# Second FFN stage in two passes of 26 products of three row groups, with its weights streamed

## The chip, the core and the metric

The kernel runs on one core of one Trainium2 chip. The metric is device microseconds from start to end of one execution. The kernel before takes 1042.76 us (median of 3 runs, 1042.61 to 1042.82). The engines named here are PE (TensorE matmul), DVE (VectorE), ACT (ScalarE) and SP (SyncE, which issues nearly all DMAs). Each takes its own instructions strictly in the order in which the program wrote them; they are tied together by semaphores.

## The reference

```python
scores = scale * np.matmul(q, k.transpose(0, 1, 3, 2)) - np.log(S)     # 8 batches, 12 heads, S = 448, D = 64
attn = 1.0 / (1.0 + np.exp(-scores))
x = np.matmul(attn, v)               # then (8 * 448, 768)
h = x @ w_in                         # 768 -> 2048
g = np.maximum(0.01 * h, h)
return g @ w_out                     # 2048 -> 768
```

All inputs are float32. The second FFN stage is the last product, `g @ w_out`.

## The kernel before

Three stages follow each other on PE: sigmoid attention over 48 pairs of heads, the first FFN stage (`h`, four passes of two batches each) and the second FFN stage (four passes of two batches each). A float32 product is made from three fp32r products: each operand is split into a high part (a cast, on ACT) and a low part (the value less its high part, on DVE), and high by high, high by low and low by high are summed in PSUM. So each operand that PE reads costs one ACT and one DVE instruction first.

Both FFN stages use fewer block products than the plain scheme, at the price of sums of blocks. The first one has 7 products for 8. The second one (`PRODUCTS`, L48) cuts `g` of two batches in 8 blocks, and `w_out` in blocks and sums of blocks, and has 20 products for the plain 24. A row of `PRODUCTS` names a stored form of `w_out`, a PSUM accumulator ("chain" A to E), the operand made of `g` (a block, or a sum or difference of two), and the results that read the chain's partial sum once the product is done. One product is 2 halves of 12 matmuls of 128 by 448 columns.

**Preparation of the weights** (`prep`, L367). Both weight matrices come as float64 bits. DVE turns them into float32 (five instructions on each of four pieces of a unit) and forms sums of blocks: `firsts` (L316) for `w_in`, `second` (L327) for `w_out`. Raw blocks and sums are stored to DRAM (`t0`, `t1`) and read back by the stages. There are 8 units of `w_in`, then 8 of `w_out`. A unit's converted blocks (`wd`) and its sums (`ws`) each take one of the two buffers of tag "w", so the next unit's `wd` takes the buffer of this unit's `wd`. `prep` is a generator: each `yield` ends one DVE instruction or is an empty step; `WAIT` = 9 empty steps follow each unit. In the attention stage `prepare` (L424) takes steps at the rate of `PACES` for the five slots of a round (one round is two pairs of heads), as long as an estimate of DVE's queue leaves room; in the first FFN stage `fill` (L432) takes up to four steps per half product. It thereby settles at which place of DVE's order each preparation instruction stands, between those of attention (`qks`, the low part of q and k of a later pair, and `x`, one of the two copies of the result out of PSUM).

**The sums of `g`**. The first FFN stage stores `g` to DRAM (`gd`), with six sums or differences of blocks (`MADE`) so that the second stage need not make these.

**The second stage's order**. `use` lists 7 triples of forms of `w_out` for 4 row units; each is loaded and split once, and stays in SBUF for all four passes. Nine of these 28 tiles (`AHEAD`) are loaded and split while PE still works in the first FFN stage, with four operands (`READY`). Then for each half product `work` (L1011) records in order: sums, low and high parts of the operands two or three ahead, weights not yet loaded, the reads of the product just ended (`read`, L983), and the 12 matmuls. `g_load` (L920) issues the loads of `g` on SP, up to eight half products ahead. Results are stored by SP one slot after the last read of them.

PSUM has three double banks for chains A to C and two single ones; a chain takes the one that was given back first. The first product takes the double bank 0.

## Time and profile before

| | |
|---|---|
| median of the runs | 1042.76 us |
| the profiled execution | 1043.02 us, its span (first to last instruction) 1041.2 us |
| granted PE clock | 1.000 |
| PE busy | 1036.3 us (100%) |
| DVE busy | 817.6 us (79%) |
| ACT busy | 592.9 us (57%) |
| DMA | 294.92 MB, mean 283 GB/s |
| attention | 0 to 250.0 us |
| first FFN stage | 250.0 to 653.3 us |
| second FFN stage | 653.3 to 1037.4 us, then the last reads and stores |

Views of the profile that are quoted later: "groups" has a row for all instructions of one kind with their count, then busy us and mean ns of one, then the idle time before them; "timeline" has a start, a duration, the instruction and, in brackets, the idle time before it with what ended it; "stages" has for each stretch the busy us of PE, PE's weight loads, DVE, ACT and POOL with the number of instructions, then clock, DMA share and GB/s; "DMA issues" has count, KB of each and the median us from issue to landing.

### The profile page before, as it was taken

How to read it: one execution, taken by the hardware profiler on the slowest of the kernel's cores; microseconds unless marked ns; L12 is line 12 of the kernel's file. 1: busy time of each engine (PE TensorE's matmuls, PEld its weight loads, DVE VectorE, ACT ScalarE, POOL GpSimd, SP SyncE). 2: the span in 40 equal slices, each digit the busy share in tenths (PEclk: the TensorE clock that was granted, in tenths of full speed). 3: DMA queues.
4: the chain of work that ended last, by engine and by line, in shares of the span. 5: the costliest groups of instructions: out<-in, count | busy, mean ns of one | idle time of the engine just before them, and what ended most of it. 6: DMA issues, size and time to landing. Idle time of an engine off the chain costs nothing.

```text
span 1041.2 us, 15783 instructions
## 1 busy us (share of the span) xinstructions
PE 1036.3 (100%) x5786; PEld 872.3 (84%) x5786; DVE 817.6 (79%) x1081; ACT 592.9 (57%) x706; POOL 0.3 (0%) x5
## 2 busy tenths in 40 slices
PE   9999999999999999999999999999999999999998
PEld 5545555556999999999999999999999999999997
DVE  4778888678988898889666558899876797678675
ACT  6778787777545555555555555566354345434442
POOL 0000000000000000000000000000000000000000
PEclk9999999999999999999999999999999999999999
DMA  8888787878789798889767898999976796688674
GB/s 301 285 280 288 256 282 260 295 251 293 259 299 314 267 326 295 305 306 346 247 228 251 285 352 286 368 352 333 335 252 223 274 340 223 233 292 286 219 268 173
DMA packets 115837, 294.92 MB, mean 283 GB/s; under 512 B 11568, under 2 KB 41264, under 8 KB 115760
## 3 DMA queue, kind: packets, MB, share of 16 engines
q1 hardware_dynamic: 114032, 290.01, 79.7%
q10 hardware_dynamic: 1728, 3.90, 1.0%
q8 instruction: 46, 0.75, 0.3%
q14 instruction: 31, 0.25, 0.1%
HBM read 207.22 MB, written 86.64 MB: 282 GB/s over the span
## 4 chain that ended last, share of the span: by engine, by line
PE 99%; ACT 0%; ACTq 0%; DVE 0%; DVEq 0%; issue 0%
PE px_h L110 22%; PE pv L110 13%; PE sc L110 11%; PE acc_B L110 11%; PE acc_A L110 11%; PE pz_h L110 11%; PE acc_D L110 6%; PE acc_C L110 6%; PE py_h L110 6%; PE acc_E L110 4%; ACTq L110 0%; ACT L110 0%; DVE o L110 0%; ACT qks L110 0%; DVEq L1086 0%
## 5 line engine op out<-in xcount | busy, mean ns | idle before, releaser
L110 PE MATMUL px_h<-hi,w 128*128 128x448 f32 x768 | 223.2, 361 | 0.0
L110 PEld LDWEIGHTS px_h<-hi,w 128*128 128x128 f32 x768 | 143.9, 187 | 11.3 <-issue 0.7
L110 DVE TENSOR_TENSOR w<-wx,w 128x768 fp32r<-128x768 f32 x112 | 106.9, 954 | 45.0 <-ACT w L110 45.0
L110 PE MATMUL px_h<-lo,w 128*128 128x448 f32 x384 | 139.4, 363 | 0.0
L110 ACT ACTIVATE s<-sc 128x896 f32<-128x896 f32 x144 | 119.5, 934 | 9.7 <-PE sc L110 9.7
L110 ACT CAST gh<-gf 128x896 fp32r<-128x896 f32 x72 | 67.7, 945 | 86.5 <-DVE gf L110 43.1
L110 ACT CAST gh<-g 128x896 fp32r<-128x896 f32 x80 | 74.1, 942 | 74.3 <-PE acc_A L110 21.8
L110 PE MATMUL pv<-s,v 128*64 128x448 f32 x576 | 113.8, 543 | 0.0
L110 PE MATMUL pz_h<-hi,w 128*128 128x448 f32 x384 | 112.7, 361 | 0.0
L110 PE MATMUL acc_A<-gh,w 128*128 128x448 f32 x384 | 111.4, 361 | 0.0
L110 PE MATMUL acc_B<-gh,w 128*128 128x448 f32 x384 | 110.8, 361 | 0.0
L110 PEld LDWEIGHTS sc<-qks 64*128 64x128 f32 x876 | 80.7, 189 | 23.1 <-issue 16.9
L110 DVE TENSOR_TENSOR g<-g,gh 128x896 fp32r<-128x896 f32 x80 | 85.6, 1087 | 18.3 <-ACT gh L110 17.0
L110 PE MATMUL sc<-qks 64*128 64x448 f32 (+1 forms) x876 | 95.6, 369 | 0.1
L110 DVE TENSOR_TENSOR gf<-g,g 128x896 f32<-128x896 f32 x80 | 86.9, 1087 | 9.3 <-DMA g<-g 2.7
L110 ACT ACTIVATE c_h<-c_h 128x896 f32<-128x896 f32 x48 | 45.8, 954 | 81.4 <-DVE c_h L110 81.4
L110 PEld LDWEIGHTS pv<-s,v 128*64 128x64 f32 x576 | 39.1, 137 | 63.3 <-issue 53.9
L110 ACT CAST w<-wx 128x768 fp32r<-128x768 f32 x112 | 91.4, 833 | 0.0
L110 DVE TENSOR_TENSOR g<-gf,gh 128x896 fp32r<-128x896 f32 x72 | 78.2, 1086 | 2.3 <-ACT gh L110 2.0
L110 PEld LDWEIGHTS acc_A<-gh,w 128*128 128x128 f32 x384 | 72.0, 188 | 5.4
L110 PEld LDWEIGHTS acc_B<-gh,w 128*128 128x128 f32 x384 | 71.9, 187 | 5.4
L110 PEld LDWEIGHTS pz_h<-hi,w 128*128 128x128 f32 x384 | 71.9, 187 | 5.3
(79 smaller groups left out, 1701.3 us busy)
## 6 DMA issues: line engine op xcount, KB each, us to landing
g<-g SPq DMA_DIRECT2D x200, 448.0 KB, 5.2
wx<-t SPq DMA_DIRECT2D x112, 384.0 KB, 4.9
g<-c_h SPq DMA_DIRECT2D x60, 448.0 KB, 4.3
qk<-in_qk SPq DMA_DIRECT2D x46, 448.0 KB, 5.1
g<-s SPq DMA_DIRECT2D x45, 448.0 KB, 5.2
wr<-in_w_in SPq DMA_DIRECT2D x32, 384.0 KB, 4.6
wr<-in_w_out SPq DMA_DIRECT2D x32, 384.0 KB, 4.3
out<-o SPq DMA_DIRECT2D x23, 448.0 KB, 3.3
```

Source lines behind the costliest of these rows:

```text
L110: return lambda *args, **kw: tc.keep_in_program_order(issue(*args, **kw))
```

## The change

The second stage now takes four batches in a pass and has two passes. A pass has 26 products of 24 forms of `w_out`. One product covers three row groups of 128 at once (`m` in 0 to 2) and all four units `e` of the contraction, so it has 3 x 4 x 3 = 36 matmuls of 128 by 448. The two chains A and B ("lanes") alternate, each with one PSUM tile of three banks; most products add to what the lane holds (third field False), and a result reads a lane between two products. An operand is a sum of up to three stored blocks or sums, or of the operand of one or two products before (`<1`, `<2`).

The weights of a product are one tile of 128 x 1536. It is loaded for each of the 52 products anew, five products ahead, and split into high (ACT) and low (DVE) each time. Six tiles are in turn: three (`t2a`) stand free in the first FFN stage and are filled and split there, three (`t2b`) lie in memory that the first FFN stage gives back. Two operands (`READY`) are made beforehand.

`second` forms eight sums into `ws`, changes two blocks of `wd`, stores both, takes nine empty steps, changes all eight blocks of `wd` in place, and stores `wd` again: 18 DVE instructions of 192 elements for nine of 128 to 256. `PACES` are about 1.35 times as large. The first FFN stage makes 5 sums of `g` for an even and 8 for an odd pass, where it made 6.

```diff
-AHEAD = 9
-GG, OO, FAR, SPARE = 10, 8, 8, 3
-READY, LEAD = 4, 2
-
-PACES = 4, 5, 4.2, 2.8, 2
+AHEAD, FAR, SPARE = 5, 6, 1
+GG, OO, WW = 7, 8, (3, 3)
+READY, LEAD = 2, 2
+
+PACES = 5.5, 6.5, 5.5, 3.7, 2.7
 TIMES = 1.92, 1.92, 2.33, 2.33, 1.66
...
+STEPS = (
+    ("sum", "s0", 1, "d1", -1, "d7"), ("sum", "s1", -1, "d2", 1, "d4"), ("sum", "s2", -1, "d2", -1, "d3"),
...
+    ("sum", "s6", -1, "d5", 1, "s3"), ("sum", "s7", -1, "s1", 1, "s0"), ("sum", "d2", 1, "d2", -1, "d0"),
+    ("sum", "d7", -1, "d6", -1, "d7"), ("store", "s", 0, 8, 0), ("store", "d", 0, 8, 8), ("wait",),
+    ("sum", "d5", 1, "d7", 1, "d5"), ("sum", "d6", -1, "d2", -1, "d6"), ("sum", "d4", -1, "d4", -1, "d5"),
...
+    ("sum", "d3", 1, "d5", -1, "d6"), ("sum", "d1", -1, "d2", 1, "d1"), ("store", "d", 0, 8, 16))
...
+        for what, *x in STEPS:
+            if what == "wait":
+                yield from (None for _ in range(WAIT))
+            elif what == "store":
+                side, i, n, form = x
+                dma(out=t2d[:, form:form + n, e, at:at + size], in_=both[side][:, i:i + n])
...
+    psum = banks("ps_o", dict(A=(1, 3), B=(1, 3), one=(2, 1)))
...
+    for k in range(total):
+        p, i = divmod(k, NF)
+        _, lane, begins, _, reads = PRODUCTS[i]
+        ending = k == total - 1
         def work():
...
+            for x in operands[k:k + 3]:
+                if x.hi and not x.has_low:
+                    x.low()
+            if k:
+                read(k - 1)
+            for x in operands[k:k + 4]:
+                if x.x is None:
+                    x.whole()
+                    x.high()
+            for x in weights[WW[0]:k + 4]:
+                if k and not x.has_high:
+                    x.high()
+                elif x.has_high and not x.has_low and x.k < k + 3:
+                    x.low()
...
+            for m in range(NM):
+                todo = [(e, part, n) for e in range(KQ) for part, n in ((0, 0), (0, 1), (1, 0))]
+                acc = accs[lane][0][m]
                 for at, (e, part, n) in enumerate(todo):
-                    mm(banks_of[m], lhsT=w2[g, h * KS + e].of(form, part, m), rhs=(me.hi, me.lo)[n][:, e],
-                       start=begins and at == 0, stop=h == 1 and at == len(todo) - 1, skip_group_check=True)
+                    mm(acc, lhsT=w.of(part, e, m), rhs=(me.hi, me.lo)[n].t[:, e],
+                       start=begins and at == 0, stop=at == len(todo) - 1, skip_group_check=True)
...
+            if WW[0] <= k + AHEAD < total:
+                weights[k + AHEAD].load()
+            g_load(k)
```

How this moves instructions is shown at three places. In these rows the name left of the arrow is written and the one right of it read; DVE_49, PE_49, Activation_49 and DMAHW0_49 to DMAHW7_49 are the semaphores that the instruction waits for, the last eight those of DMAs.

The first place is DVE in the attention stage, in the middle of the preparation of the first unit of `w_out`. Before, from the last sums of the unit to the next unit:

```order
L110 TENSOR_TENSOR ws1_0_2333<-wd1_0_2190 128x2x128
L110 TENSOR_TENSOR ws1_0_2333<-ws1_0_2333 128x2x128 [waits DVE_49]
L110 TENSOR_TENSOR ws1_0_2333<-wd1_0_2190,ws1_0_2333 128x2x128
L110 TENSOR_TENSOR ws1_0_2333<-ws1_0_2333,wd1_0_2190 128x128 [waits DVE_49]
L110 TENSOR_TENSOR ws1_0_2333<-ws1_0_2333 128x128
L110 TENSOR_TENSOR qks_40_2423<-qk_40_2271,qks_40_2423 128x832 [waits DMAHW3_49,PE_49,Activation_49]
```

Now, from the last sum into `ws` over the two changed blocks of `wd`, the nine empty steps and the changes in place:

```order
L127 TENSOR_TENSOR ws1_0_2091<-ws1_0_2091 128x192
L127 TENSOR_TENSOR wd1_0_1922<-wd1_0_1922 128x192
L127 SCALAR_TENSOR_TENSOR wd1_0_1922<-wd1_0_1922 128x192 [waits DVE_49]
L127 TENSOR_TENSOR wd1_0_1922<-wd1_0_1922 128x192 [waits DMAHW7_49,DVE_49]
L127 TENSOR_TENSOR qks_34_2129<-qk_34_1979,qks_34_2129 128x832 [waits DMAHW6_49,PE_49,Activation_49]
L127 SCALAR_TENSOR_TENSOR wd1_0_1922<-wd1_0_1922 128x192
L127 SCALAR_TENSOR_TENSOR wd1_0_1922<-wd1_0_1922 128x192 [waits DVE_49]
L127 TENSOR_TENSOR wd1_0_1922<-wd1_0_1922 128x192
L127 SCALAR_TENSOR_TENSOR wd1_0_1922<-wd1_0_1922 128x192 [waits DVE_49]
L127 TENSOR_TENSOR qks_35_2148<-qk_35_2044,qks_35_2148 128x832 [waits DMAHW1_49,PE_49,Activation_49]
```

The fourth of these rows is the first one after the empty steps. It waits for a DMA semaphore, that of the second store; no other DVE instruction stands between it and the row before it, and the low parts of two pairs of heads stand behind it.

The second place is SP where the first FFN stage ends. It now reads, from the last store of this stage on SP to the loads of the second stage's weights (`g` are loads of operands, `t1` the stored forms of `w_out`):

```order
L127 DMA g_3_15_123<-s7_3_2_6269 128x896 [waits DMAHW4_49,DVE_49]
L127 DMA g1s0_2_6350<-g_1_8_87 128x1792 [waits DMAHW6_49,PE_49]
L127 DMA g111_3_6421<-g_1_5_84 128x1792 [waits DMAHW2_49]
L127 DMA g001_4_6423<-g_0_1_67 128x1792 [waits DMAHW3_49]
L127 DMA g011_4_6425<-g_0_5_71 128x1792 [waits DMAHW1_49,DMAHW5_49,DMAHW0_49,DMAHW7_49,DVE_49,Activation_49]
L127 DMA g1s4_4_6427<-g_1_12_91 128x1792 [waits DMAHW4_49]
L127 DMA g1s7_5_6429<-g_1_15_94 128x1792 [waits DMAHW5_49,DMAHW2_49]
L127 DMA w1_3_6431<-t1_61 128x1536 [waits DMAHW3_49,PE_49]
L127 DMA w1_4_6433<-t1_61 128x1536
L127 DMA w1_5_6476<-t1_61 128x1536
```

The weights of the fourth product, `w1_3`, stand behind three loads of operands, the first of which (`g011_4`, into memory that the first FFN stage gives back) waits for four DMA semaphores. These are of the last stores of the first FFN stage, which are on ACT's queue (`ends` in `after`).

The third place is SP at the very end, where the last results are stored:

```order
L127 DMA out_0<-o1_010_7747 128x224 [waits DMAHW0_49,DVE_49]
L127 DMA out_0<-o1_010_7747 128x224 [waits DMAHW2_49,DVE_49]
L127 DMA out_0<-o1_010_7747 128x224 [waits DMAHW4_49,DVE_49]
L127 DMA out_0<-o1_000_8383 128x3x448 [waits DMAHW6_49]
L1125 UNCONDITIONAL_BRANCH
```

Before, the last row ahead of the branch was a piece of 128 x 224; now a whole result, `o1_000`, follows the three pieces of the last product.

More of the change, by code (lines that the diff above doesn't have):

```diff
@@ L652, in advance, with __init__ @@
             at_load += 1
+    class Results(dict):
+        def __init__(self):
+            self.planned = set()
     class First:
@@ L709, in after @@
             z = LATER if u == NU // 2 - 1 else 0
-            for i, x in enumerate(x for x in MADE if name(row, col) in x and set(x.replace("-", "+").split("+")) <= set(c)):
-                later(2 + i + z, lambda x=x: made(x))
+            have = set(c)
+            i = 0
+            for x in MADE[p % 2]:
+                if x[0] not in c.planned and {x[2], x[3]} <= have | c.planned:
+                    c.planned.add(x[0])
+                    later(2 + i + z, lambda x=x: made(*x))
+                    i += 1
     last = B * NP - 1
@@ new lines, in whole, with free, release @@
+            for _, x in self.terms:
+                y = self.at[x]
+                if x[0] == "<":
+                    y.release()
+                else:
+                    y.free(x, self.dead)
+        def free(self, x, to):
+            self.count[x] -= 1
+            if self.count[x] == 0:
+                to.append(self.raw[x])
+        def release(self):
+            self.uses -= 1
+            if self.uses == 0:
+                if self.single:
+                    y, x = self.own
+                    dead = []
+                    y.free(x, dead)
+                    for h in dead:
+                        h.drop()
+                else:
+                    self.held.drop()
@@ new lines, in high @@
+        def high(self):
+            self.hi = self.dead.pop() if len(self.dead) > 1 else Held(f"gh_{self.k}")
+            copy(out=self.hi.t, in_=self.x)
+        def low(self):
+            y, x = self.own if self.single else (None, None)
+            inside = self.single and self.uses == 1 and y.count[x] == 1
+            self.lo = y.raw[x] if inside else self.dead.pop() if self.dead else Held(f"gl_{self.k}")
+            for h in self.dead:
+                h.drop()
+            sub(self.lo.t, self.x, self.hi.t)
+            if inside:
+                y.count[x] = 0
+            else:
+                self.release()
@@ L931, in attn_ffn_kernel @@
[L931 to L946 removed]
+    weights = [Wide(k, t2a) for k in range(WW[0])]
@@ L947, in attn_ffn_kernel @@
+    todo = [(operands[k], "load") for k in range(READY)]
+    for k in range(READY):
+        todo += [(operands[k], what) for what in ("whole", "high", "low")]
+    todo += [(operands[READY], "load")]
+    ahead = READY + 1
+    for k in range(NOP, size):
+        m, at = divmod(k - NOP, 12)
+        if m < WW[0] and at == 0:
+            for n, what in ((0, "load"), (5, "high"), (7, "low")):
+                later(n, getattr(weights[m], what))
         if k >= size - LEAD - len(todo) and todo:
-            later(0, lambda x=todo.pop(0): g_step(*x))
+            later(0, lambda x=todo.pop(0): getattr(*x)())
@@ L960, in attn_ffn_kernel @@
[L960 to L970 removed]
+    spare.extend((op, f"o{n}") for n in range(8))
@@ new lines, in store, with take, read @@
+        dma(out=place(p, o).rearrange("m p s -> p m s"), in_=outs.pop((p, o)))
+    def take(how, t, acc):
+        if how == "c":
+            copy(out=t, in_=acc)
+            return
+        a, b = (acc, t) if how == "r" else (t, acc)
+        (add if how == "+" else sub)(t, a, b)
+    def read(k):
+        p, i = divmod(k, NF)
+        for x in PRODUCTS[i][4]:
+            how, o = x[0], x[1:4]
+            if how == "c":
+                outs[p, o] = outp.tile([P, NM, S], F32, tag="out", name=f"o{p}_{o}")
+            for rows, acc in accs[PRODUCTS[i][1]][1]:
+                take(how, outs[p, o][:, rows], acc)
+            if x[4:]:
+                later(1, lambda o=o: store(p, o))
```

331 lines of the change are left out of this document (127 added, 204 removed), and 20 rows, old and new, of tables (PRODUCTS, STEPS).

## The prediction

> **What bounds the kernel now.** The page's first lines come first, then the chain of work that ended last, then a table by stage.
>
> ```profile
> span 1041.2 us, 15783 instructions
> PE 1036.3 (100%) x5786; PEld 872.3 (84%) x5786; DVE 817.6 (79%) x1081; ACT 592.9 (57%) x706; POOL 0.3 (0%) x5
> ```
>
> ```profile
> 1023.11 9.60 PE acc_B L110 x48
> 1032.71 4.81 PE acc_D L110 x24
> ```
>
> ```profile
> 150.00:200.00 50.00, 50.00 (x376) 26.45 (x374) 42.33 (x81) 39.08 (x49) 0.00 (x0) 1.00 0.84 283
> 300.00:400.00 100.00, 100.00 (x502) 93.73 (x501) 88.08 (x122) 55.01 (x63) 0.00 (x0) 1.00 0.88 304
> 653.00:700.00 47.00, 47.00 (x237) 44.05 (x236) 40.83 (x44) 28.17 (x34) 0.00 (x0) 1.00 1.01 376
> 653.30:1037.40 384.10, 384.10 (x1922) 359.77 (x1920) 302.75 (x305) 177.63 (x204) 0.00 (x0) 1.00 0.78 280
> ```
>
> The chain is PE alone, with no gap in any stage; 48 matmuls in 9.60 us are 0.200 us each. So each matmul removed is worth 0.2 us, and each wait that reaches PE costs its full length, because PE has no idle time to take it from. DVE is busy 85% in attention (42.33 of 50), 88% in the first FFN stage and 79% in the second (302.75 of 384.10): it runs close behind, and what it does later than now PE will soon feel.
>
> **PE's own work.** Before, 4 passes x 20 products x 24 matmuls = 1920; now 2 x 26 x 36 = 1872. 48 fewer at 0.200 us: **-9.6 us**, if nothing else moves. Column count and type of a matmul stay, so its price does too.
>
> **The preparation's wait in attention.** The rows on `wd1_0` in the first order piece show what is new. Two stores of 128 x 8 x 192 floats (786 kB, 768 KB in the profile's unit) leave within two DVE instructions of each other, and then DVE wants to overwrite what the second one reads. The nine empty steps are meant as distance, but they cost DVE nothing: at the new paces they pass within two slots, and between the two rows no DVE instruction stands. So DVE stands still until the second store has landed, and `qks`, which PE's next scores read, stands behind.
>
> ```profile
> t<-ws SPq DMA_DIRECT2D x7, 768.0 KB, 4.8
> ```
>
> ```profile
> 115.20 1.02 DVE L110 TENSOR_TENSOR qks<-qk,qks 128x832 fp32r<-128x832 f32 x1
> 117.67 1.02 DVE L110 TENSOR_TENSOR qks<-qk,qks 128x832 fp32r<-128x832 f32 x1
> 118.62 3.91 PE L110 MATMUL sc<-qks 64*128 64x448 f32 x36
> ```
>
> ```profile
> L110 DVE TENSOR_TENSOR ws<-ws 128x256 f32<-128x256 f32 (+1 forms) x16 | 5.7, 355 | 0.3
> ```
>
> The first store (DMA issues, 50 to 250 us) takes 4.8 us from issue to landing. The second queues behind it: 786 kB at the 376 GB/s of the 653 to 700 row, where the DMA engines are full, are 2.1 us, so it lands 6.9 us after the first was issued. DVE works for two sums more after that issue (355 ns each): it stands still for 6.9 - 0.7 = 6.2 us. How early are the low parts now? In the timeline the first one ends at 116.22 and PE starts on the pair's scores at 118.62, 2.4 us of lead. So PE waits 6.2 - 2.4 = 3.8 us for the first pair. For the second pair DVE has five sums (about 0.3 each when they follow each other) and a low part of 1.0 to do while PE does half of 3.91 us: 0.9 us more, with 0.1 for the semaphores. 4.7 us a place. Units 0 to 3 of `w_out` stand in attention with the same rows (in the fourth, one of the two low parts stands ahead of the wait), so four places: **+18.8 us**. Bounds: 10 us, if the second store lands no later than a single one (4.8 - 0.7 = 4.1 us still, 2.6 a place), and 30 us, if landings are those of a full queue (7.5 us in the row on `w<-t` below; 8.9 us still, 7.4 a place). Four measured landings at that size lie next to the middle, so I take that.
>
> [...]
>
> Units 4 to 7 stand in the first FFN stage. There one to seven other DVE instructions stand between the two, and the low parts of weights are made two to three steps of nine matmuls (1.8 us each) ahead. I take 0; with that lead gone it would be up to 2 us a unit. The larger work itself (18 sums of 192 for 9 of up to 256, some 2 us more a unit, and four more sums of `g`, 1.09 each) is hidden behind PE: DVE has 7 of 50 us free in the attention row and 12 of 100 in the other.
>
> **Where the second stage begins.** T is the last matmul of the first FFN stage, 653.3 us in the timeline before.
>
> ```profile
> 653.54 0.92 ACT L110 ACTIVATE c_h<-px_h 128x896 f32<-128x896 f32 x1 [1.52 <-PE px_h L110]
> 653.61 1.21 ACTq L110 DMA_DIRECT2D g<-c_h  x2
> 654.91 3.60 ACTq L110 DMA_DIRECT2D g<-s  x3
> ```
>
> ```profile
> w<-t SPq DMA_DIRECT2D x13, 384.0 KB, 7.5
> g<-s ACTq DMA_DIRECT2D x3, 448.0 KB, 5.8
> ```
>
> ```profile
> L110 DVE TENSOR_TENSOR lo<-x,hi 128x1344 fp32r<-128x1344 f32 x24 | 37.3, 1553 | 1.2 <-ACT hi L110 1.2
> L110 DVE TENSOR_TENSOR g<-g,gh 128x896 fp32r<-128x896 f32 x80 | 85.6, 1087 | 18.3 <-ACT gh L110 17.0
> L110 ACT CAST hi<-x 128x1344 fp32r<-128x1344 f32 x24 | 31.8, 1326 | 2.7 <-PE py_h L110 2.7
> L110 ACT CAST w<-wx 128x768 fp32r<-128x768 f32 x112 | 91.4, 833 | 0.0
> ```
>
> (a) The first accumulator now covers three banks, among them that of the last `px`, which ACT reads until T + 1.1: PE waits **1.1 us** for it. Before, the first product took a bank pair that was free. (b) From these groups, along a straight line: DVE 2.02 us for 1792 elements and 1.75 for 1536, ACT 1.71 and 1.49. ACT has two casts and three copies of 1344 (7.4 us) ahead of the third product, the copies not before T + 8.3, and that product, on the same lane, is due at T + 15.5. If the casts start with the stores' end at about T + 9, they are done at T + 16.4: 0 to 1 us, I take **0.8**. (c) SP's load `g011_4` waits for the last stores on ACT's queue. The last sum of these is the fourth on DVE after T + 1.1, so at T + 5.3, and it lands 5.8 us later, at T + 11.1. Behind it on SP are three loads of 917 kB and then `w1_3` (786 kB): 3.5 MB at 376 GB/s are 9.4 us, and about 2 us for the landing itself, so T + 22.6. A cast of 1.49 and a low part of 1.75 follow, T + 25.9; PE wants it at T + 23.5. That is 2.4 us, and up to 4.4 where DVE's sum of the next operand (2.02) goes first, as it is written: **3.5**. Together **+5.4 us**. Bounds: 1.1 (a alone) to 9 (landings of 7.5 us twice). `w1_4` and `w1_5` follow 2.1 us apart and PE takes 7.2 us a product, so nothing is late next.
>
> **Steady part.** A product now lasts 7.2 us on PE, and DVE has in each one low part of an operand and one of the weights (3.8 us), 17 sums in 26 products and about a read for each. By the durations above 332 us for all; back to back they overlap:
>
> ```profile
> 860.95 1.09 DVE L110 TENSOR_TENSOR g<-gf,gh 128x896 fp32r<-128x896 f32 x1
> 861.96 1.09 DVE L110 TENSOR_TENSOR gf<-g,g 128x896 f32<-128x896 f32 x1
> ```
>
> by 0.08 us each, so 317 of 374 us, 85% (79% now). The densest stretch, products 4 to 13, has 10 + 10 low parts, 11 sums and 9 reads: 70.7 of 72 us. Operands are made two or more products (14 us) ahead, so I take 0 here. DMA: 52 weight tiles, 62 operand loads and 16 results are 109 MB, what the stage moves now at share 0.78: 0.
>
> **The end.**
>
> ```profile
> 1037.54 0.68 DVE L110 TENSOR_TENSOR o<-o,acc_D 128x224 f32<-128x224 f32 x2 [0.52 <-PE acc_D L110]
> out<-o SPq DMA_DIRECT2D x23, 448.0 KB, 3.3
> out<-o ACTq DMA_DIRECT2D x2, 112.0 KB, 1.8
> ```
>
> In the last product the second row group adds into the same PSUM tile as the first, so it waits for the two adds that read the first: 0.68 + 0.2 = **0.9 us**. And the store of `o1_000` (688 kB) stands on SP behind the last small pieces: it takes 3.3 us plus 0.6 for its 229 kB more, where a small piece took 1.8: **+2.1**. Together **+3.0 us** (1.5 to 4).
>
> **The sum.** 1043.02 (the profiled execution: span 1041.2 and 1.8 around it) - 9.6 + 18.8 + 5.4 + 3.0 = 1060.6. The median of the runs is 0.26 below the profiled one: **1060 us**, 1.7% slower.
>
> **Rivals.**
>
> 1. The stores' wait does not reach PE: they land within the lead, or DVE catches up. For it: the queue moves 283 GB/s of the 376 it can, and DVE has 7 us in 50 free. Against: 6.2 us of standstill against 2.4 of lead. It decides when a landing is under some 3 us after the second issue. 1043.0 - 9.6 + 5.4 + 3.0 = 1041.8, less 0.3: 1041.5, no change that can be told (0.2%, 2 us, is what a measurement here can tell). Chance 0.06.
> 2. The wait at the beginning of the second stage is hidden too: then the matmuls saved show. 1043.0 - 9.6 + 3.0 - 0.3 = 1036, faster. For it: PE has been the only bound everywhere. Against: `w1_3` is issued at T + 11 at the earliest, by the order on SP. Chance 0.06.
> 3. DVE becomes the bound in the dense stretches of the second stage, on top of the forecast.
>
> ```profile
> DVE o L110 <- PE acc_B L110: 18.9, 14, 2.7
> DVE o L110 <- PE acc_A L110: 15.4, 11, 2.2
> DVE o L110 <- PE acc_C L110: 11.5, 7, 2.7
> ```
>
> By the list of waits each of these 32 reads holds DVE for 1.4 us until PE is done. Nine of them would be 13 us on 70.7 of 72: 11 us late in each of two stretches. The 14 us of lead cover that; where tiles run out and the lead is one product, 4 us show in each: 1060 + 8 = 1068. Chance 0.13.
>
> The forecast has 0.75.
>
> **Range and chances.** With B's bounds (10 to 30), C's (1.1 to 9) and the end's (1.5 to 4) the extremes are 1046 and 1076; all at one end at once is unlikely, so 1048 to 1070 for 8 in 10, which leaves out rivals 1 and 2. Faster 0.06, within 0.2% 0.05, slower 0.89.
>
> **What would show it.** On DVE in attention four idle times of 5 to 7 us, ended by a DMA that stores `wd`, each with PE idle ahead of `sc` right after; attention ends near 269 us. Later PE idle three times within 25 us of the second stage's start, then not until the last product. Wrong it would be, if DVE idles there without PE (rival 1), if `w1_3` is split before T + 23 (rival 2), or if PE idles all through the second stage (rival 3).

## The result and the profile after

The changed kernel takes 1066.9 us (median of 4 runs, 1065.7 to 1067.5), the kernel before 1042.8 (1042.6 to 1044.2): 1.0227 times as long, 95% interval 1.0209 to 1.0244. The direction was right and the time lies in the predicted range; it is 6.9 us above the predicted 1060.

```profile
span 1065.7 us, 15110 instructions
PE 1039.8 (98%) x5738; PEld 868.3 (81%) x5738; DVE 845.8 (79%) x1024; ACT 585.0 (55%) x610; POOL 0.3 (0%) x5
```

PE was busy for 1036.3 of 1041.2 us. Now it has 26 us without work, and although it has 48 matmuls less (9.6 us) its busy time is larger: some of its work ran more slowly. The list of waits of the kernel after (what waited, for what: us in total, times, longest) says where it stands still:

```profile
DVE wd L127 <- DMA t<-wd: 33.0, 8, 7.7
PE sc L127 <- DVE qks L127: 10.7, 3, 4.4
PE sc L127 <- DVE x L127: 4.9, 3, 4.3
PE acc_B L127 <- ACT o L127: 1.5, 1, 1.5
PE acc_A L127 <- ACT c_h L127: 1.0, 1, 1.0
PE acc_B L127 <- DVE o L127: 0.8, 1, 0.8
```

The first row is the wait that was predicted: DVE stands before a sum that overwrites `wd` until the store of `wd` has landed. The next two are PE behind it. The timeline at the second of the four places in attention (start, us, instruction; in brackets the idle time before it and what ended it), with PE's scores of an undisturbed round (two pairs of heads, 36 matmuls) in the first two rows:

```profile
198.19 3.90 PE L127 MATMUL sc<-qks 64*128 64x448 f32 x36
202.02 2.48 PE L127 MATMUL pv<-s,v 128*64 128x448 f32 x12
...
208.34 0.47 PE L127 MATMUL sc<-qks 64*128 64x448 f32 x2
210.81 0.36 DVE L127 TENSOR_TENSOR wd<-wd 128x192 f32<-128x192 f32 x1 [6.59 <-DMA t<-wd]
211.09 1.02 DVE L127 TENSOR_TENSOR qks<-qk,qks 128x832 fp32r<-128x832 f32 x1
212.16 5.42 PE L127 MATMUL sc<-qks 64*128 64x448 f32 x34 [3.36 <-DVE qks L127]
217.51 0.97 PE L127 MATMUL pv<-s,v 128*64 128x448 f32 x4
```

DVE stands still for 6.59 us; `qks` follows it, as the program has it, and PE, which can do only the two matmuls on high parts, waits 3.36 us. But look at the last duration too: 34 of the 36 matmuls take 5.42 us, where 36 take 3.83 in the undisturbed round. The table of stretches of 3.41 us (us, PE busy, granted clock, share of the DMA engines, GB/s) shows why:

```profile
180.89:184.30 3.41, 1.58 (x18) 1.00 0.98 276
184.30:187.72 3.42, 2.29 (x12) 0.50 0.25 93
187.72:191.13 3.41, 3.41 (x18) 0.50 0.38 117
...
208.20:211.61 3.41, 0.61 (x6) 1.00 0.98 287
211.61:215.02 3.41, 2.86 (x16) 0.50 0.12 38
...
235.50:238.92 3.42, 0.02 (x2) 1.00 0.39 138
238.92:242.33 3.41, 3.34 (x16) 0.50 0.01 2
...
262.81:266.22 3.41, 0.69 (x8) 1.00 0.99 330
266.22:269.64 3.42, 1.80 (x10) 0.50 0.47 185
269.64:273.05 3.41, 3.41 (x18) 0.50 1.02 282
```

After each of the four waits the granted clock in the trace is 0.50, for one or two such stretches (6.8, 3.4, 3.4 and 6.8 us), 20.5 us in all. This was not in the prediction.

The whole difference, from the two timelines:

| part | us | how it is measured |
|---|---|---|
| attention ends (first `px_h`) at 277.8 instead of 250.0 | +27.8 | the four places cost 25.0 (first score to first `pv`, less the 3.83 us of an undisturbed round: 6.0, 5.3, 6.6 and 7.0, the last with 0.8 for the half clock that runs on behind it), the start of the execution 1.5, two small waits 0.6, 0.7 unassigned |
| first FFN stage, 403.7 instead of 403.5 | +0.2 | first `px_h` to the end of the last |
| matmuls removed | -9.6 | 48 x 0.200 |
| start of the second stage | +3.5 | the fifth product starts at 713.8; 681.5 + 4 x 7.2 would be 710.3 |
| steady part | 0 | next fence |
| end | +2.5 | 1.0 in the last product, 1.5 behind the last matmul (5.2 instead of 3.7) |
| sum | +24.4 | the spans differ by 24.5 |

From the fifth product (713.84) to the last (1052.24) there are 47 products in 338.4 us, 7.2 each and not one wait:

```profile
760.00:1060.00 300.00, 299.22 (x1497) 1.00 0.70 258
```

The 0.78 us missing here stand in the last product, behind DVE's reading of the shared PSUM tile.

### The profile page after: what moved, and what is told of

Read it like the earlier page. It is cut to its first block, busy times and chain, and to the rows that moved or that the text cites. A ratio compares the mean times of both kernels' runs of the same rounds, so it can differ in the third digit from the quotient of the medians.

```text
span 1065.7 us, 15110 instructions
## 1 busy us (share of the span) xinstructions
PE 1039.8 (98%) x5738; PEld 868.3 (81%) x5738; DVE 845.8 (79%) x1024; ACT 585.0 (55%) x610; POOL 0.3 (0%) x5
## 4 chain that ended last, share of the span: by engine, by line
PE 88%; DMA 5%; DVE 4%; issue 1%; ACT 1%; SPq 0%; ACTq 0%; DVEq 0%
PE px_h L127 22%; PE acc_B L127 17%; PE acc_A L127 16%; PE pz_h L127 11%; PE pv L127 9%; PE sc L127 8%; PE py_h L127 5%; DMA t<-wd 2%; DVE wd L127 2%; DMA w<-t 1%; DVE ws L127 1%; DVE qks L127 1%; DMA wx<-t 1%; DMA wr<-in_w_out 1%; DVE x L127 0%
## 5 line engine op out<-in xcount | busy, mean ns | idle before, releaser
L127 PE MATMUL acc_A<-gh,w 128*128 128x448 f32 x528 | 152.6, 363 | 1.0 <-ACT c_h L127 1.0
L127 PE MATMUL acc_B<-gh,w 128*128 128x448 f32 x424 | 123.0, 363 | 2.5 <-ACT o L127 1.5
L127 PE MATMUL sc<-qks 64*128 64x448 f32 (+1 forms) x876 | 105.7, 392 | 16.1 <-DVE qks L127 10.7
L127 PEld LDWEIGHTS acc_A<-gh,w 128*128 128x128 f32 x528 | 99.1, 188 | 7.8 <-ACT c_h L127 1.4
L127 DVE TENSOR_TENSOR w<-w 128x1536 fp32r<-128x1536 f32 x52 | 91.0, 1751 | 0.0
L127 PEld LDWEIGHTS acc_B<-gh,w 128*128 128x128 f32 x424 | 79.5, 188 | 8.7 <-ACT o L127 1.9
L127 PE MATMUL acc_B<-g,w 128*128 128x448 f32 x332 | 86.0, 361 | 0.0
L127 ACT CAST w<-w 128x1536 fp32r<-128x1536 f32 x52 | 76.9, 1478 | 0.7 <-DMA w<-t 0.7
L127 PEld LDWEIGHTS px_h<-lo,w 128*128 128x128 f32 x384 | 72.1, 188 | 3.8
L127 DVE SCALAR_TENSOR_TENSOR wd<-wr,wd 128x384 int32<-128x384 int32 x128 | 71.4, 558 | 3.5
```

The costliest lines, as they stand in the source:

```text
L127: return lambda *args, **kw: tc.keep_in_program_order(issue(*args, **kw))
```

## The experiments

Each kernel is the changed kernel with the edit shown, unless said otherwise. Ratios are to the kernel before, with their 95% interval.

| run | us (median) | ratio | attention ends, us | idle of DVE at the four places, us | idle of PE there, us |
|---|---|---|---|---|---|
| before | 1042.7 | | 250.0 | | |
| the change | 1066.9 | 1.0227 [1.0209, 1.0244] | 277.8 | 6.7, 6.6, 7.7, 6.0 | 15.1 |
| e1, other store | 1043.0 | 1.0004 [0.9994, 1.0014] | 251.6 | 0.3, 1.3, 1.5, 1.4 | 0.6 |
| e2, small filling | 1070.7 | 1.0268 [1.0246, 1.0290] | 280.4 | 6.6, 6.6, 7.3, 4.9 | 11.2 |
| e3, early store | 1051.7 | 1.0094 [1.0077, 1.0111] | 259.8 | 3.0, 3.0, 5.4, 2.7 | 7.2 |
| e4, twenty steps | 1058.1 | 1.0151 [1.0128, 1.0175] | 260.6 | 6.6, 7.1, 4.2, 0.4 | 7.2 |
| e5, full filling | 1064.7 | 1.0205 [1.0190, 1.0220] | 272.6 | 6.6, 6.7, 7.3, 5.7 | 5.3 |
| e6, split store | 1048.5 | 1.0049 [1.0034, 1.0064] | 259.1 | 0, 2.5, 5.5, 2.7 | 5.7 |
| e7, banks | 1067.3 | 1.0231 [1.0214, 1.0247] | 275.4 | 6.6, 6.6, 7.2, 4.8 | 14.3 |
| e8, mended | 1046.7 | 1.0034 [1.0021, 1.0047] | 255.9 | 0, 2.6, 4.6, 0.5 | 4.3 |
| e9, third buffer | 1043.4 | 1.0002 [0.9993, 1.0010] | 252.4 | 0, 0, 0, 0 | 0 |
| e10, buffer and end | 1040.3 | 0.9972 [0.9962, 0.9982] | 252.2 | 0, 0, 0, 0 | 0 |
| e11, and filling | 1039.5 | 0.9961 [0.9948, 0.9975] | 253.0 | 0, 0, 0, 0 | 0 |

### Is it the store?

```diff
-    ("store", "s", 0, 8, 0), ("store", "d", 0, 8, 8), ("wait",),
+    ("store", "s", 0, 8, 0), ("store", "s", 0, 8, 8), ("wait",),
```

> In the first order piece the store of the first eight sums of `wd` reads `ws` instead; the same bytes leave on the same queue at the same place, and every sum on DVE stays as it is. Only the dependency between that store and the sums that overwrite `wd` is gone. Stored forms 8 to 15 of w_out hold other sums than they should, so the output is not the reference's; the amount of work is that of the changed kernel. Theory A (the wait for the second store, and nothing else in the new preparation, makes attention longer): the four idles of DVE of 6 to 7.7 us go, PE's idles of 3 to 4.4 us ahead of `sc` go with them, the granted clock stays at 1.00 there, attention ends near 250 to 251 us instead of 277.8, and the time is 1039 to 1041 us. Rival (the new paces and the doubled number of DVE sums in attention make PE wait, whatever the store does): attention still ends above 265 us and the time stays above 1055 us. In between, each takes its share: 1 us of the end of attention is 1 us of the time.

1043.0 us: the whole loss is gone, by an edit that changes neither a sum on DVE, nor the number of bytes stored, nor the pace. What this kernel leaves out is eight of the stored forms, so it gives a time and not the reference's result. The list of waits of this run:

```profile
DVE wd L127 <- DMA t<-ws: 4.5, 4, 1.5
PE sc L127 <- DVE x L127: 1.0, 3, 0.4
```

DVE's four idles of 6 to 7.7 us are gone; the four short ones that are left stand before the next unit, which reuses the memory of the store's new source. Attention ends at 251.6 us. The rival, more sums and other paces as such, is refuted. The median lies 2 us above the top of what was expected; the profiled execution, with 1041.3, was the fastest of ten.

### What makes DVE's wait as long as it is?

```diff
-    ("sum", "s3", ...), ("sum", "s4", ...), ("sum", "s5", ...),
-    ("sum", "s6", ...), ("sum", "s7", ...), ("sum", "d2", ...),
-    ("sum", "d7", ...), ("store", "s", 0, 8, 0), ("store", "d", 0, 8, 8), ("wait",),
+    ("sum", "s5", ...), ("sum", "d2", ...), ("sum", "d7", ...), ("store", "d", 0, 8, 8),
+    ("sum", "s3", ...), ("sum", "s4", ...), ("sum", "s6", ...),
+    ("sum", "s7", ...), ("store", "s", 0, 8, 0), ("wait",),
```

> The steps in the first order piece are reordered, none is added or taken away: the sums s5, d2 and d7 that complete `wd` come first, then its store, then the other four sums of `ws` and its store, then the empty steps. So `wd`'s store is the first of the two on the queue and has four sums of DVE (about 1.1 to 1.4 us) and not one behind it before DVE needs its memory. By the theory that DVE waits for the second of two queued stores: its wait should fall from 6.7 to between 3 and 4 us (one store's 4.4 to 4.8 us less four sums), below what PE has in lead plus what sets the clock down: PE idle under 1.5 us at each place, no half clock, attention ends near 251 to 257 us, and the time is 1040 to 1047. If the wait were for the landing of both stores whatever their order, or the DVE work, the time stays above 1060.

1051.7 us, 15 less. With the store of `wd` first on the queue and four sums of distance, DVE's waits fall to 3.0, 3.0 and 2.7. At the third place it is 5.4: there SP had been held up by another store until 214.2 us, four loads went out right behind that, and the store of `wd`, issued at 218.4, took 6.4 us instead of the 3.9 at the first place. PE's waits for `sc` in this run:

```profile
PE sc L127 <- DVE x L127: 6.0, 6, 1.6
PE sc L127 <- DVE qks L127: 2.2, 1, 2.2
```

Each wait of DVE costs PE that wait less 1.5 to 2.1 us (2.96 gave 0.91, 2.97 gave 1.44, 5.42 gave 2.18 + 1.63, 2.72 gave 1.05), and the clock stays at 1.00 throughout attention. What PE waits for is, but for the 2.18 us, no low part. It is DVE's copy `x` of an earlier result out of PSUM, whose tile the next scores take (scores and results share the four PSUM tiles of one tag); the low part had been done 1.1 to 1.3 us earlier. The copy stands behind the low parts in DVE's order and comes late with them, with a lead of 1.5 to 2.1 us. The low part has more lead: at the first three places after the change PE waited 2.96, 3.36 and 4.43 us for it where DVE stood still for 6.71, 6.59 and 7.67, so 3.2 to 3.8 us less.

The time was 5 us above the expected range. Attention ends 2.8 us above its own expected range, with the third place and the late copies in it; and in the profiled execution the clock is halved from 688.7 to 692.1 us, at the start of the second stage, which costs 1.7 us more. In the kernel after, the issues in the stretch of the first place show the two stores as they were predicted (KB, us from issue to landing):

```profile
t<-ws SPq DMA_DIRECT2D x1, 768.0 KB, 3.9
t<-wd SPq DMA_DIRECT2D x1, 768.0 KB, 6.6
```

They were issued at 176.86 and 177.40, so the second lands 7.1 us after the first was issued and 3.2 us after the first has landed; these 3.2 us are the part that an earlier place on the queue takes away.

The other way to get distance is more empty steps:

```diff
-                yield from (None for _ in range(WAIT))
+                yield from (None for _ in range(20 if u < 4 else 9))
```

> The empty steps between the store and the sums that overwrite `wd` are 20 instead of nine in the four units of w_out that stand in attention; at the paces there that is about two more slots of the emission, so that one or more `qks` of a later pair of heads stand on DVE between the store and the waiting sum. By the theory (the empty steps cost DVE nothing unless other DVE work falls into them): DVE has 1 to 4 us of other work before it waits, the wait is 6.7 less that, PE is idle under 2 us at each place, and the clock holds: attention ends at 250 to 262 us and the time is 1039 to 1052. If what DVE stands for is not distance to the store, the time stays above 1060.

1058.1 us, outside the expected range. At the first two places DVE still waits 6.6 and 7.1 us with nothing in between: there the twenty steps fall between two `qks`, and no other work of DVE comes up. At the third and fourth it waits 4.2 and 0.4. So an empty step is distance only where other DVE work happens to be due. In the first FFN stage this kernel loses 3.5 us more in one wait of PE for `c_h`: DVE had stood 6.47 us there until a store of sums of `g` landed. How the edit leads to that wait was not tried.

Splitting the store lets the blocks that no sum of the first group changes leave ten sums earlier:

```diff
+    ("store", "d", 0, 2, 8, 1), ("store", "d", 3, 4, 11, 1),
...
+    ("sum", "d2", ...), ("sum", "d7", ...), ("store", "d", 2, 2, 10, 5),
...
-    ("store", "d", 0, 8, 8), ("wait",),
+    ("store", "s", 0, 8, 0, 1), ("wait",),
```

> `wd` is stored in three pieces: its blocks 0 and 1 and its blocks 3 to 6, which no sum of the first group changes, right after they are decoded; blocks 2 and 7 after their two sums, which now come before four of the sums of `ws`. The same bytes and the same sums; the first sums that overwrite `wd` now find a store that was issued ten sums and two slots earlier. By the theory that the wait for the store is the whole of what attention lost: DVE waits under 2 us at each of the four places (up to 4 at one of them, where the stores queue behind other transfers on SP), PE idle under 1 us a place, no half clock, attention ends at 251 to 256 us, time 1042 to 1048. If the wait is for the queue's whole backlog rather than for a store's own place in it, little changes: above 1055.

1048.5 us, half a us above the expected range. The first place has no wait any more; the others keep 2.5, 5.5 and 2.7. At the third place the pieces, issued from 216.9 on behind the same loads, took 6.9 and 7.3 us (medians of the pieces of 192 and of 384 KB) where they took 2.8 and 2.9 at the first. There the earlier issue still left 5.5 us of DVE's wait (7.7 after the change), with the queue behind: both halves of the expectation are partly right, the store's own place and the queue's backlog.

### What does the half clock cost?

```diff
                for n, (c, ps) in enumerate(acts):
+                if h == 0 and n == 0 and self.i in (34, 38, 42, 47):
+                    for _ in range(3):
+                        for j, me in enumerate(heads):
+                            for rows in heads:
+                                mm(ps[rows, j, :S], lhsT=self.raw[me, 1, S - D:], rhs=self.raw[me, 0], ...)
```

> Twelve small fp32 matmuls (64 x 64, on the raw queries and keys, which lie ready) are put ahead of the first scores of the four pairs of heads where PE stood still; they write into the tile that the real scores then start afresh. DVE's wait for the store is untouched, so the scores can begin no earlier than now; PE has about 0.5 to 2.5 us more to do at each place. Theory A (PE's stand-still itself costs 16 us, and on top of it the granted clock is halved for some us after each: four times, 20 us of half clock in all, 10 us lost): with PE idle for a shorter stretch the clock stays at 1.00 after the places, and the time falls by 6 to 10 us, to 1057 to 1061, although work is added. If only some of the places keep their clock, by 1.7 us (where the half clock lasted 3.4) or 3.4 us (where it lasted 6.8) for each. Rival (the halved clock is not set off by PE's stand-still there, or costs nothing because PE waits for others then anyway): same time within 1 us, or up to 5 us more.

1070.7 us: not faster, as the rival said, but the run does not decide. At the first two places the clock stayed at 1.00, and they cost 4.9 and 5.5 us instead of 6.0 and 5.3; at the third it was halved all the same; at the fourth the filling was put ahead of the wrong pair, came after the wait and ran at half clock itself. It showed one thing: with the clock held PE meets a second wait of 1.44 us, for the copy `x`, which the half clock had covered. So the filling was made of full matmuls, and put where PE stands:

```diff
                for n, (c, ps) in enumerate(acts):
+                for j in range({34: 12, 38: 14, 42: 18, 46: 18}.get(self.i, 0) if h == n == 0 else 0):
+                    mm(ps[:, j % 2, :S], lhsT=self.parts[:, 0, 1, :P], rhs=self.parts[:, 0, 0], ...)
```

> The first filling used quarter-size matmuls and left the clock halved at two of four places. Now 12, 14, 18 and 18 matmuls of 128 x 128 with 448 columns (0.2 us each, so 2.4, 2.8, 3.6 and 3.6 us) stand ahead of the first scores of the pairs where PE stood still 2.96, 3.36, 4.43 and 4.34 us; the real scores then start the same tile afresh. DVE's waits stay. Theory A1 (each halving costs its full half, 10 us in all): the clock stays at 1.00 and the time falls by about 10 us, to 1057. Theory A2 (with the clock held, PE meets the second low part of the pair, which DVE delivers late anyway; in the run with the earlier store each wait of DVE cost PE that wait less 1.7 us and the clock never fell): the four places then cost 6.7, 6.6, 7.7 and 6.0 less 1.7 each, 20.2 us, where they cost 25.3 now, so the time falls by about 5 us, to 1061 to 1063. Rival (the clock has nothing to do with PE's stand-still): the clock falls as before and the time stays or rises by up to 3 us.

The timeline of PE at the second place of this run with two rows of DVE, and its table of stretches there and at the start of the second FFN stage:

```profile
204.93 3.51 PE L127 MATMUL sc<-qks 128*128 128x448 f32 x16
208.85 1.89 PE L127 MATMUL sc<-qks 64*128 64x448 f32 x16 [0.41 <-DVE qks L127]
209.91 1.01 DVE L127 TENSOR_TENSOR qks<-qk,qks 128x832 fp32r<-128x832 f32 x1
211.50 0.61 DVE L127 COPY x<-pv 128x448 f32<-128x448 f32 x1
212.17 2.09 PE L127 MATMUL sc<-qks 64*128 64x448 f32 x18 [1.44 <-DVE x L127]
214.19 2.10 PE L127 MATMUL pv<-s,v 128*64 128x448 f32 x10
```

```profile
208.07:211.48 3.41, 2.25 (x18) 1.00 0.14 52
211.48:214.90 3.42, 2.73 (x22) 1.00 0.46 145
...
699.59:703.00 3.41, 0.83 (x3) 1.00 1.02 422
703.00:706.41 3.41, 3.41 (x10) 0.50 1.03 425
```

The clock is 1.00 all through attention, with DVE's waits nearly unchanged (6.6, 6.7, 7.3, 5.7, in sum 0.7 us less): the clock went with PE's standing still, 5.3 us there in place of 15.1, and not with DVE's. The four places now cost 4.9, 5.4, 6.2 and 4.3 us, 20.8 in place of 25.0. So the half clock cost 3.5 to 4.2 us there (4.2, of which up to 0.7 can be DVE's shorter waits), not the 10.2 that half of 20.5 us would be: the rest of it lay over the second wait. That is theory A2 in its size (20.2 and 25.3 were expected), but not in its reason: the second low part ends at 210.92 and PE goes on at 212.17, 0.06 us after the copy `x`. To move that copy was not tried. Of the gain the whole kernel shows only 2.2 us, 1064.7: in this run the wait ahead of the fourth product of the second stage was 2.80 us (1.50 after the change), and a halved stretch followed it there, 1.7 us.

The same test at that other place, on the faster kernel e10 (below): seven matmuls of 0.2 us between the third and the fourth product, into a tile that nobody reads.

```diff
+            if k == 2:
+                t = psum("one", "fill")
+                for e in range(7):
+                    mm(t[:, :S], lhsT=w.of(0, e % KQ, 0), rhs=me.hi.t[:, e % KQ], ...)
```

> The kernel of the run before, and seven matmuls of 128 x 128 with 448 columns (1.4 us in all) between the third and the fourth product of the second stage, into a PSUM tile that nobody reads: PE stands still there for 1.67 us (ahead of the fourth product's accumulator) and 0.21 us, and in the profiled execution the clock was halved for the 3.41 us after. Nothing else is changed; DVE and ACT get no more to do, and the fourth product can begin no earlier. Theory (PE's idle share of a 3.41 us window sets the clock for the next window: every window of these traces with over 1.85 us of idle was followed by a halved one, none with under 1.65 us): idle falls to about 0.5 us, the clock stays at 1.00 in the second stage, and the time falls by up to 1.7 us, to 1038.6 to 1039.6 (one execution of seven of the kernel before this had no halving to lose). Rival (the halved clock there has another cause, the start of the stage's transfers for one, or PE must wait for DVE's low parts afterwards anyway, as it did in attention): the time stays at 1040 to 1041.

1039.5 us (1040.3 without it). The stretches of e10 around the wait, and those of e11:

```profile
677.85:681.26 3.41, 1.71 (x8) 1.00 1.02 420
681.26:684.67 3.41, 3.24 (x9) 0.50 1.04 428
```

```profile
676.76:680.17 3.41, 3.41 (x19) 1.00 1.02 425
680.17:683.58 3.41, 3.19 (x15) 1.00 1.01 418
```

The fourth product's low part comes no later (25.2 us after the end of the first FFN stage, 25.4 in e10), but PE works until then, and the clock stays at 1.00. The mean clock is 1.000 in all five executions; without the filling it is 0.998 in six of seven, which is what one halved stretch makes (1.7 of 1038.9 us). From the end of the first FFN stage to the last matmul it takes 377.9 us instead of 379.6 in the profiled executions. So useless work saves 1.7 us in this stretch. Of the whole kernel's time the gain by the medians is 0.8 of the expected 1.7 us, and the intervals of the two ratios overlap: that the kernel as a whole is faster by it is not shown beyond the spread of the runs.

### The start and the end of the second stage

```diff
+    for name in ("B", "one"):
+        psum(name, "banks")
```

> Only the places of the accumulators change: lane B's and the single one's tiles are placed first, so that the first product of the second stage gets banks that the last `px` of the first stage does not have. The first accumulation then starts 1.0 us earlier. Theory (a, the prediction's sum: its 1.1 us stands by itself): PE's 1.0 us ahead of `acc_A` goes, the later waits of 1.50 and 0.20 us stay as they are, and the fifth product starts 1.0 us earlier relative to the end of the first FFN stage (31.3 us after it instead of 32.3). Theory (b, one chain: the fourth product's weights and the copies ahead of it on ACT have a fixed time after the last stores of the first stage, so PE gets there earlier and waits longer): the 1.0 us goes and the wait at the fourth product grows from 1.7 to 2.7 us, and the fifth product starts as late as now. Either way the total is within 1.5 us of the changed kernel, so the places in the trace decide, not the time.

PE's rows with a wait at the start of the second stage in the timeline, after the change and in this run:

```profile
682.51 0.47 PE L127 MATMUL acc_A<-gh,w 128*128 128x448 f32 x1 [1.01 <-ACT c_h L127]
705.89 0.47 PE L127 MATMUL acc_B<-gh,w 128*128 128x448 f32 x1 [1.50 <-ACT o L127]
706.77 0.68 PE L127 MATMUL acc_B<-gh,w 128*128 128x448 f32 x2 [0.20 <-DVE w L127]
```

```profile
693.85 0.47 PE L127 MATMUL acc_A<-gh,w 128*128 128x448 f32 x1 [0.36 <-ACT o L127]
703.54 0.47 PE L127 MATMUL acc_B<-gh,w 128*128 128x448 f32 x1 [2.21 <-ACT o L127]
704.41 1.12 PE L127 MATMUL acc_B<-gh,w 128*128 128x448 f32 x2 [0.19 <-DVE w L127]
```

The 1.01 us are gone, and 0.36 at the third and 0.7 more at the fourth product come in their place. The third row stands 25.3 us after the end of the first FFN stage in both (681.5 and 679.1). That is theory b, one chain: what PE saves ahead of it, it waits there. The fifth product even starts 1.5 us later than before the edit, counted from the end of the first FFN stage, because the 2.21 us wait is followed by a halved stretch (704.2 to 707.6). ACT's rows after the change show what the chain is:

```profile
701.30 1.48 ACT L127 CAST w<-w 128x1536 fp32r<-128x1536 f32 x1 [0.25 <-DMA w<-t]
703.18 1.48 ACT L127 CAST w<-w 128x1536 fp32r<-128x1536 f32 x1 [0.40 <-DMA w<-t]
704.57 1.27 ACT L127 COPY o<-acc_B 128x1344 f32<-128x1344 f32 x1
```

The copy that empties the second product's accumulator stands behind the casts of the fourth and fifth product's weights, and these wait for their loads, which stand on SP behind the load that waits for the first stage's last stores.

All mends at once, before the banks were understood:

```diff
+    ("store", "d", 0, 2, 8, 1), ("store", "d", 3, 4, 11, 1),        (as in e6)
-                yield from (None for _ in range(WAIT))
+                yield from (None for _ in range({2: 16, 3: 6}.get(u, WAIT)))
-                dma(out=xd[half - KEPT], in_=xs[half])
+                dma_act(out=xd[half - KEPT], in_=xs[half])
+    for name in ("B", "one"): psum(name, "banks")                   (as in e7)
-            for x in weights[WW[0]:k + 4]:
+            for x in weights[WW[0]:k + (4 if k > 1 else 3)]:
...
+                if k == total - 1: store(p, o)
...
```

> The changed kernel with all of it mended: `wd` stored in three pieces; the empty steps 16 and 6 in the third and fourth unit instead of nine; one attention result stored on ACT's queue, so that it does not hold up SP ahead of the third unit's stores; the accumulators' banks as in the run before; the casts of the fifth product's weights one product later on ACT; and the store of `o1_000` ahead of the last pieces instead of behind them. By the theory (attention's loss is the store wait, and 9.6 us of PE work are really gone): attention ends at 250 to 253 us, the start of the second stage costs 2 to 4 us, the tail behind the last matmul is 3.7 to 4.2 us instead of 5.2, and the time is 1037 to 1042 us: at or below the kernel before. If PE's gain is eaten by something that these edits leave, it stays at 1043 or above.

1046.7 us; the expected 1042 was missed. The stores still land late at two places (2.6 and 4.6 us of DVE); at the start of the second stage PE waits 0.77 and 2.03 us, and the 2.03 us, which lie within one stretch, were followed by a stretch at 0.50; the first FFN stage is 1.3 us longer; and the edit for the last store tested the wrong product number, so the store stayed where it was and the tail at 5.2 us.

Instead of getting the store away sooner, its memory can be left alone. In attention there is room for a third buffer:

```diff
+    apart = attn.enter_context(tc.tile_pool(name="apart", bufs=1, reuse_waits="tile"))
...
+        if u < 4:
+            t = apart.tile([P, 4 * HW], F32, tag="x", name=f"wx1_{u}")
+            both["x"] = t.rearrange("p (n m) -> p n m", n=n)
-        for what, *x in STEPS:
+        for what, *x in STEPS[:-9] + APART if u < 4 else STEPS:
```

(`APART` is the last nine steps with the blocks of `x` written in place of those of `d`.)

> In the four units of w_out that are prepared in attention, the last eight sums go to a buffer of their own (6 KB a partition, which attention has free) instead of overwriting `wd`; the same sums, stores and order otherwise. No sum on DVE then needs memory that a store still reads. By the theory (the store wait is the whole of what attention lost): as with the other source of the store, attention ends 1 to 2.5 us later than in the kernel before, at 249 to 253 us, no half clock in attention, and the time is 1041 to 1045 us, no different from the kernel before by more than 0.2%: the 9.6 us that PE saves go into the start of the second stage (2.7 us of PE's idle, and 1.7 us more where a half clock follows it), the end (2.4 us) and 1 to 2.5 us of attention. If the overwriting cost more than its wait, the time would fall under 1040.

1043.4 us, 1.0002 [0.9993, 1.0010], as expected. PE waits for `sc` 1.5 us in all of attention:

```profile
PE sc L131 <- DVE x L131: 1.5, 2, 1.3
```

This is the change without its fault, and it is no faster than the kernel before: of the 9.6 us saved 2.4 go into attention, 0.2 into the first FFN stage, 5.2 into the start of the second (the fifth product starts at 690.1 instead of 656.1 + 28.8; 1.7 of it are a halved stretch) and 2.5 into the end, and the spans differ by 0.7. For the end:

```diff
-                later(1, lambda o=o: store(p, o))
+                if k == total - 2:
+                    store(p, o)
+                else:
+                    later(1, lambda o=o: store(p, o))
...
-                    t, one = psum(lane, f"acc_{lane}{k}"), psum("one", f"acc_one{k}")
+                    t, *one = psum(lane, f"acc_{lane}{k}"), psum("one", f"acc_one{k}a"), psum("one", f"acc_one{k}b")
...
```

> The kernel of the run before, and two edits at the end: the store of `o1_000` is issued ahead of the pieces of the last product (the edit meant for this in the mended kernel tested the wrong product number, and its trace still shows the 672 KB store last), and the three row groups of the last products have a PSUM tile each, so that PE need not wait for DVE's reading of the first. By the trace of the change: the tail behind the last matmul falls from 5.2 us to 3.7 to 4.2, and PE's 0.78 us ahead of the second row group goes. Together 1.8 to 2.6 us less than the run before: 1039 to 1043 us, and faster than the kernel before by 0.1 to 0.3%. If the tail is set by the last pieces' own stores whatever stands ahead of them, the tail stays at 5.2 us.

1040.3 us, 0.9972 [0.9962, 0.9982]: faster than both kernels. The wait of 0.78 us is gone, and behind the last matmul there are 3.3 us (1035.6 to 1038.9) where there were 5.2. With e11's filling it is 1039.5, 0.9961 [0.9948, 0.9975].

## Why the prediction was right, and where it was off

- **PE's own work, -9.6:** right; the steady part runs at 7.2 us a product, 0.200 a matmul as before, without a wait.
- **The preparation's wait in attention, +18.8:** the mechanism is right (e1 and e9 take it away, and the loss with it). DVE stood still for 6.0 to 7.7 us where 6.2 was predicted. At the first place the landings came 3.9 and 7.1 us after the first issue where 4.8 and 6.9 were taken: the first store was quicker and the second added 3.2 us, not 2.1. Two small terms were near: sums of 192 that follow each other start 0.27 us apart (176.21, 176.48, 176.75) where 0.3 was taken, and PE went on 0.05 us after the low part (212.11 to 212.16, second place) where 0.1 was taken for the semaphores. With the clock held the four places cost 20.8 us (e5), half a us a place more than predicted. That the two come so near is luck in part. PE's first wait was DVE's less 3.2 to 3.8 us, where the sum took 2.4 off. And the 0.9 us for the second pair's low part (0.6 by the prediction's own 0.3 us a sum) stood for a wait that is not there: that low part was in time, and PE waited 1.4 to 1.6 us for the copy `x`, which the prediction did not name. The term that was missing is **the clock**: a place was reckoned as idle time alone, and the half clock behind it adds 3.5 to 4.2 us in all. The rest of the 27.8 is the start of the execution (1.5, see the last section), 0.6 in two small waits and 0.7 unassigned.
- **Where the second stage begins, +5.4:** 3.5 measured. (a) 1.1 predicted, 1.01 measured, but e7 shows that it is no term of its own: without it PE waits as much later. (b) put the wait at the third product; that one ran through, and it was the fourth that stood behind ACT, 1.50 us. The three waits are 2.7 us together; the other 0.8 lies in the first matmul after each of them, which takes 0.47 us where one in the stream adds 0.20. (c) gave 3.5 for the late weights; their low part came only 0.20 us late, because they were landed at 701.3, 19.8 us after the end of the first stage, not 22.6. The 2 us in it for the landing itself were an estimate; the row of 112 KB has 1.8, and at the end of the kernel after such a store took 1.7. The cause named in (c), the queue behind the first stage's last stores, is seen in ACT's rows; that it alone sets the 25.3 us was not tried.
- **Steady part 0 and rival 3:** the 0 was right, and the rival is refuted. DVE is busy 251.4 of 300 us there (84%), and PE waits for it nowhere.
- **The end, +3.0:** 2.5 measured (0.9 predicted for the shared tile, 1.0 measured; 2.1 for the last store, 1.5 measured). e10 takes both away.
- **Rivals 1 and 2:** both would need a landing within PE's lead; DVE waited 3.6 to 5.3 us longer than the 2.4 that were taken for it.

Together attention took 9.0 us more than forecast, and the start and the end of the second stage 2.4 us less, so part of the miss is cancelled.

The landing of one store was not steady either: the first store took 3.9 us at the first place, 6.05 at the third and 4.41 at the fourth.

## What to carry to other kernels

Here an in-place update behind a store stood 6.0 to 7.7 us, until that store had landed behind the one queued ahead of it (3.9 and 7.1 us after the first issue at the first place): count what the engine itself has to do in between, not how many scheduling steps, and spend a buffer before spending order. A stall of the matrix engine is to be priced with the clock behind it: each of the four stalls was followed by 3.4 or 6.8 us at 0.50, and that cost 3.5 to 4.2 us in all, half of the 20.5 us less what PE would have waited for anyway. Where an engine stands still, look at every instruction behind it that another engine waits for, and not only at the first one: here the copy `x` had a lead of 1.5 to 2.1 us, the low parts 3.2 to 3.8. And the start that one chain set gave nothing back when one of its waits was removed: 1.01 us went in e7, and 1.06 came in their place.

## What the runs showed of the hardware

**The granted clock.** The trace of an execution records the granted clock, 1.00 or 0.50 here, with the time of each change, and what follows was measured in these records and in PE's rows. After the change the stretches at 0.50 in attention last 6.83, 3.41, 3.41 and 6.83 us, and those at 1.00 between them 20.48, 23.89 and 23.89: 2, 1, 1, 2 and 6, 7, 7 times 3.413 us. In the 13 profiled executions every change lies on such a grid of 3.413 us, at a phase of its own: 10.2, 180.9 and 208.2 us are on it after the change, 677.9 in e10, 676.8 in e11. Sorted by PE's idle time in a stretch at full clock (from 12 us to the end of the last matmul, stretches with at least 0.3 us of it):

| idle in a stretch of 3.41 us, clock 1.00 | stretches | next stretch halved |
|---|---|---|
| 0.3 to 1.63 us | 74 | 0 |
| 1.68 to 1.83 us | 8 | 5 |
| 1.89 us and more | 15 | 15 |

A halved stretch was followed by another where PE was idle 0.65 us or more in it (7 of 7; 1.12 and 1.61 us after the change), and by full clock at 0.55 us or less. A wait of 2.2 us that straddles two stretches was followed by no halved one (2.18 in e3, whose clock is 1.00 throughout attention, and 2.2 in e6, with a mean clock of 1.000); of the waits of 0.77 and 2.03 us in e8, each within one stretch, the second was: its stretch has 1.38 us of PE's work in 3.41, and the next one 0.50. The first place in attention fell to half with 2.96 us of idle in all, of which 1.83 lay in the stretch before the fall. How the chip comes to set it, no run shows.

**The start of an execution varies.** The timeline of the first pairs, before and after the change:

```profile
7.54 0.98 PE L110 MATMUL sc<-qk 64*64 64x448 f32 x8
10.86 2.09 PE L110 MATMUL sc<-qks 64*128 64x448 f32 x18
```

```profile
8.12 1.77 PE L127 MATMUL sc<-qk 64*64 64x448 f32 x8
12.40 2.09 PE L127 MATMUL sc<-qks 64*128 64x448 f32 x18
```

The same eight matmuls take 1.77 us instead of 0.98, and the second pair starts 1.5 us later: the trace records the full clock from 10.2 us on, and before the change from 6.9. In the 13 executions that point lies between 4.3 and 10.5 us, in kernels whose first pairs do the same work. At 1.77 us for the work of 0.98, about half of such a difference is lost, so up to 3 us of a time of this kernel can be decided there (an estimate, half of the 6.2 from 4.3 to 10.5): a single execution does not show 1.5 us of anything.
